# Load order, normalisation and transposes in the opening of a fused attention and feed-forward kernel

## The chip, the cores and the metric

The kernel runs on one core of one Trainium2 chip. The metric is the device time of one execution in microseconds (us), the median of several executions. The engines are PE (TensorE matmul), PEld (its weight load), DVE (VectorE), ACT (ScalarE), POOL (GpSimd) and SP, which here issues DMA transfers.

## The reference

Two rounds of a linear attention block and a bilinear feed-forward block, each on a layer norm of the residual stream (S = 2048 tokens, D = 1024, 32 heads, F = 3584):

```python
def _A_ref(x, wqkv, wo):                       # x: 1 x 2048 x 1024
    qkv = (x @ wqkv)                           # q, k, v; 32 heads of 32
    phi = lambda t: jnp.where(t > 0, t + 1, jnp.exp(t)) + 1e-6
    pq, pk = phi(q), phi(k)
    kv = jnp.einsum("bhsd,bhse->bhde", pk, v)  # one 32 x 32 matrix per head
    z = jnp.einsum("bhsd->bhd", pk)
    num = jnp.einsum("bhqd,bhde->bhqe", pq, kv)
    den = jnp.einsum("bhqd,bhd->bhq", pq, z)[..., None] + 1e-6
    return (num / den) @ wo
def _B_ref(x, w_gate, w_up, w_down):
    return ((x @ w_gate) * (x @ w_up)) @ w_down
x = x + _A_ref(_layernorm(x), wqkv, wo)
x = x + _B_ref(_layernorm(x), w_gate, w_up, w_down)
x = x + _A_ref(_layernorm(x), wqkv, wo)        # the same weights again
x = x + _B_ref(_layernorm(x), w_gate, w_up, w_down)
```

## The kernel before

A small scheduler records operations per engine. Every engine runs its own operations in the order in which they were recorded, and waits by semaphore for what an operation reads. So the order of the recording calls below is the program order of each engine. The 2048 tokens are 16 tiles of 128. The change touches only the opening of the first attention layer.

The loads go out in this order (`x0` in two halves comes first; a "half" of the key or query weights is 1 MB, a token tile 256 KB):

```python
load_w("k", 0)
xload(1)
load_w("k", 1)
xload(2)
load_w("q", 0)
xload(3)
load_w("q", 1)
for i in range(4, NST):
    xload(i)
```

The layer norm of one tile has three parts on DVE and POOL, and then its transposes:

```python
def ln_a(i):                      # statistics
    ...
    for h in range(2):
        P.add("dve", ... e.bn_stats(...) ...)      # half of the columns each
    P.add("dve", ... e.bn_aggr(...) ...)
    P.add("pool", ... add eps ...); P.add("pool", ... pow -0.5 ...)
    return j
# ln_b2: normalise, one tensor_scalar on DVE, f16 output
def transpose(self, n):
    if self.use_dma:
        P.add("sp", lambda e: e.dma_start_transpose(xnT[...], d), ...)
        return
    if self.to == "A0" and n == 0:                 # tile 0: two halves, two PSUM banks
        for hf, b in enumerate((B_TP, B_KQ[3])):
            P.add("pe", ... 4 transposes ...)
            P.add("act", ... e.copy(...) ...)
        return
    P.add("pe", ... 8 transposes ...)
    P.add("act", ... e.copy(...) ...)
```

The opening itself, and the loop over the first ten tiles' key and query projections (8 matmuls of 128x512 for each half):

```python
NHOLD = 2; NPL1 = 10; NPE_T = 6
def lnstep(i, h):                                  # called after key half h of tile i
    if h == 0:
        if lnp.n < NST:
            lnp.start(lnp.n)                       # statistics of one more tile
        lnp.b_one()                                # normalise one
    else:
        lnp.use_dma = i + 1 >= NPE_T               # later tiles: transposes by DMA
        lnp.step_t(1)                              # transpose one
lnp.start(0); lnp.b_one(); lnp.start(1); lnp.step_t(1); lnp.b_one(); lnp.start(2)
...
twk = tw_make("k", "dve", 1); twq = tw_make("q", "dve", 1)   # weight differences
seq = [("k", i) for i in range(NHOLD)]
for i in range(NHOLD, NPL):
    seq += [("q", i - NHOLD), ("k", i)]
...
for kind, i in seq:
    for h in range(2):
        ev = proj(kind, tok[i], h)                 # 8 matmuls on PE
        ev()                                       # exp, relu on ACT, combine on DVE
        if kind == "k":
            lnstep(i, h)
    if kind == "q" and i >= 1 and len(twk) > 1:
        twk.pop(0)()
    elif kind == "q" and i >= 1 and len(twq) > 1:
        twq.pop(0)()
    ...
```

The weight differences (`twk`, `twq`) are subtractions of weight blocks on DVE, 1.22 us each by the source view (the prediction reads 1.13 from the chain view). The next stage, which computes two tiles at a time with 7 block products in place of 8, reads them.

## Time and profile before

| | before |
|---|---|
| median of 3 runs | 1440.06 us (1439.99 to 1440.2) |
| span of the profiled run | 1438.3 us |
| PE busy | 1421.8 us, 16.5 us idle |
| first key product starts | 7.85 us |
| third key product starts | 14.74 us |
| first product of the next stage | 82.48 us |

Lines such as L891 are lines of the kernel. Between the two kernels they shift: the projections are L891 before and L907 after, the next stage L920 and L939, the transposes L546/L554 and L557/L565, the attention output L1242 and L1275, the gate and up products L1324 and L1357. Idle time in brackets is the idle time of that engine just before the group, and what is named after the arrow is what ended it. The clock in a table of stretches is that of PE, with 1.00 as full speed. The prediction below shows the lines of the profile and reads them.

### The profile page before, as it was taken

What the parts mean: (1) busy time and instruction counts of PE and PEld (TensorE: products, weight loads), DVE (VectorE), ACT (ScalarE), POOL (GpSimd) and SP (SyncE); (2) the same over time, 40 slices, a digit from 0 to 9 for tenths busy, and PEclk for the clock granted to TensorE, in tenths of its full rate; (3) what the DMA queues carried; (4) which work ended last, traced back from release to release, by engine and by line L of the source; (5) the groups of instructions that cost most, each with busy time, mean ns of one, the idle gap of its engine ahead of it and who ended that gap; (6) DMA issues with size and microseconds to landing.
All of it is one profiled execution on the core that took longest, in us unless ns stands there. A gap on an engine that the chain in (4) does not pass through costs nothing.

```text
span 1438.3 us, 21791 instructions
## 1 busy us (share of the span) xinstructions
PE 1421.8 (99%) x8126; PEld 787.8 (55%) x8186; DVE 1213.8 (84%) x2376; ACT 680.2 (47%) x1389; POOL 148.9 (10%) x176
## 2 busy tenths in 40 slices
PE   8999999999999999999999999999999999999999
PEld 3444444555545666664544444446666475666547
DVE  6987977999978799988779978778888887888888
ACT  5663255444420266662148823567776004777400
POOL 2212621000010000002000045310000100000000
PEclk9999999999999999999999999999999999999999
DMA  8477978997785777777984266757775976777653
GB/s 263 88 205 220 213 173 182 302 298 266 263 268 199 249 254 249 255 251 270 260 265 108 86 170 151 191 177 262 253 260 191 283 255 224 264 260 257 206 193 120
DMA packets 270458, 320.21 MB, mean 223 GB/s; under 512 B 161936, under 2 KB 212880, under 8 KB 270352
## 3 DMA queue, kind: packets, MB, share of 16 engines
q1 hardware_dynamic: 270352, 318.82, 72.2%
q8 instruction: 64, 1.05, 0.3%
q14 instruction: 42, 0.34, 0.1%
HBM read 236.45 MB, written 73.40 MB: 215 GB/s over the span
## 4 chain that ended last, share of the span: by engine, by line
PE 87%; DVE 7%; DMA 2%; issue 2%; ACT 1%; POOL 0%; SPq 0%; DVEq 0%; ACTq 0%
PE ps L1324 28%; PE ps L1741 17%; PE ps L1405 17%; PE ps L1140 8%; PE ps L920 6%; PE ps L1659 5%; PE ps L1242 4%; PE ps L891 3%; DVE arena L766 2%; DVE arena L451 1%; DMA arena<-arena 1%; DVE arena L769 1%; DVE arena L613 1%; DMA arena<-in_A_wqkv_dram 1%; PE ps L1166 0%
## 5 line engine op out<-in xcount | busy, mean ns | idle before, releaser
L766 DVE TENSOR_TENSOR arena<-arena 128x512 f16<-128x512 f16 (+8 forms) x1015 | 497.8, 518 | 59.8 <-ACT arena L1409 34.1
L1324 PE MATMUL ps<-arena 128*128 128x512 f16 x1888 | 457.2, 379 | 1.8 <-DVE arena L769 1.0
L769 DVE SCALAR_TENSOR_TENSOR arena<-ps,arena 128x512 f16<-128x512 f32 (+3 forms) x545 | 353.9, 664 | 69.4 <-PE ps L1741 28.4
L1405 PE MATMUL ps<-arena 128*128 128x256 f16 x2184 | 287.5, 273 | 1.0 <-DVE ps L1418 1.0
L1324 PEld LDWEIGHTS ps<-arena 128*128 128x128 f16 (+1 forms) x1888 | 182.9, 98 | 164.4 <-ACT ps L1353 3.8
L1405 PEld LDWEIGHTS ps<-arena 128*128 128x128 f16 (+1 forms) x2184 | 212.2, 98 | 91.6 <-ACT arena L1409 6.9
L1741 PE MATMUL ps<-arena 128*128 128x512 bf16 (+1 forms) x1102 | 242.6, 379 | 0.9
L1741 PEld LDWEIGHTS ps<-arena 128*128 128x128 f16 x1120 | 109.6, 98 | 130.2
L1329 ACT ACTIVATE arena<-ps 128x512 f32<-128x512 f32 x224 | 133.8, 597 | 76.5 <-PE ps L1324 61.7
L1409 ACT ACTIVATE arena<-ps 128x256 f32<-128x256 f32 x351 | 125.1, 384 | 26.9 <-PE ps L1405 22.0
L920 PE MATMUL ps<-arena 128*128 128x512 f16 (+1 forms) x551 | 122.4, 379 | 2.0 <-ACT arena L617 0.7
L1140 PE MATMUL ps<-arena 128*128 128x512 bf16 x498 | 114.7, 379 | 0.7
L1242 PE MATMUL ps<-arena 128*128 128x512 bf16 x502 | 110.5, 379 | 0.7 <-DVE arena L1248 0.2
L454 POOL TENSOR_SCALAR arena<-arena 128x1 f32<-128x1 f32 x64 | 24.8, 388 | 821.6 <-DVE arena L453 821.6
L1415 ACT COPY ps<-ps 128x256 f32<-128x256 f32 x182 | 66.3, 364 | 74.6 <-DVE arena L769 28.3
L1353 ACT COPY ps<-ps 128x512 f32<-128x512 f32 x112 | 65.4, 583 | 65.0 <-PE ps L1324 51.9
L451 DVE BATCH_NORM_STATS2 arena<-arena 128x6 f32<-128x512 bf16 x128 | 88.2, 689 | 8.9 <-DMA arena<-in_A_x_dram 6.7
L1022 POOL TENSOR_TENSOR arena<-arena 128x1024 f16<-128x1024 f32 x32 | 77.2, 2414 | 156.4 <-DVE arena L1020 142.0
L920 PEld LDWEIGHTS ps<-arena 128*128 128x128 f16 x560 | 53.9, 98 | 69.5 <-ACT arena L927 5.2
L891 PE MATMUL ps<-arena 128*128 128x512 bf16 x375 | 84.6, 379 | 4.2 <-ACT arena L556 1.6
L1659 PE MATMUL ps<-arena 128*128 128x256 f16 (+1 forms) x784 | 86.8, 273 | 0.3 <-ACT ps L1672 0.2
L1418 DVE TENSOR_TENSOR ps<-ps,arena 128x256 f32<-128x256 f32 x182 | 76.7, 428 | 10.5 <-PE ps L1405 9.5
(61 smaller groups left out, 905.9 us busy)
## 6 DMA issues: line engine op xcount, KB each, us to landing
arena<-w_scratch SPq DMA_DIRECT2D x84, 896.0 KB, 4.6
arena<-t_scratch SPq DMA_DIRECT2D x32, 896.0 KB, 5.8
arena<-in_B_w_down_dram SPq DMA_DIRECT2D x24, 896.0 KB, 4.9
arena<-sp_scratch SPq DMA_DIRECT2D x26, 768.0 KB, 4.3
w_scratch<-arena SPq DMA_DIRECT2D x28, 512.0 KB, 6.3
arena<-w_scratch SPq DMA_DIRECT2D x28, 384.0 KB, 5.0
x_scratch<-arena SPq DMA_DIRECT2D x40, 256.0 KB, 7.4
arena<-x_scratch SPq DMA_DIRECT2D x40, 256.0 KB, 5.9
```

The costliest lines, as they stand in the source:

```text
L766: P.add("dve", lambda e: e.tensor_tensor(out=out, in0=a, in1=b, op=op), rd=rd, wr=wr, prd=prd)
L769: P.add("dve", lambda e: e.scalar_tensor_tensor(out=out, in0=a, scalar=sc, in1=b, op0=ALU.mult, op1=op1), rd=rd, wr=wr, prd=prd)
L891: return [e.matmul(psb(bank), xnT[:, k, i * 128:(i + 1) * 128], t[:, k, h * 512:(h + 1) * 512], start=(k == 0), stop=(k == KT - 1)) for k ...
L920: P.add("pe", lambda e: [e.matmul(psb(bank), a[0][:, k, :], b[0][:, k, :], start=(q in (1, 5) and k == 0), stop=(k == 3), skip_group_check ...
L1140: return [e.matmul(psb(bank), xrt[t][:, jj * 128:(jj + 1) * 128], pk[:, h, t, :], start=(t == tok[0]), stop=(t == tok[NST - 1])) for t in ts]
L1242: return [e.matmul(psb(bank), xnT[:, g, i * 128:(i + 1) * 128], wp[:, g, dh * 512:(dh + 1) * 512], start=(dh == 0 and g == 0), stop=(g == ...
L1324: P.add("pe", lambda e: [e.matmul(psb(bank), w[:, k, :], x[:, k, :], start=(start and k == 0), stop=(k == 3), skip_group_check=True) for k ...
L1329: P.add("act", lambda e: e.activation(t, psb(bank), AF.Copy, scale=SG), prd=[bank], wr=r)
L1405: P.add("pe", lambda e: [e.matmul(psb(bank)[:, 256 * half:256 * half + 256], w[:, k, :], xx[:, k, :], start=(start and k == 0), stop=(k == ...
L1409: P.add("act", lambda e: e.activation(d, src, AF.Copy, scale=sc), prd=[xk], wr=rd_)
L1659: P.add("pe", lambda e: [e.matmul(psb(bank)[:, 256 * half:256 * half + 256], a[:, k, 128 * r:128 * r + 128], b[:, k, :], start=(start and ...
L1741: P.add("pe", lambda e: [e.matmul(psb(bank), hv[:, 7 * hf + k, t * 128:(t + 1) * 128], w[:, k, :], start=(q in "15" and hf == 0 and k == 0 ...
```

## The change

The intent: let PE transpose tile 1 while it would wait for the second half of the key weights anyway, keep a third key tile ahead of the first query product, give DVE work in its early idle time, and take the transposes of tiles 4 and 5 off PE. The core of the diff, with cuts:

```diff
-    NPE_T = 6
+    NPE_T = 4
...
+            def start_half(self):            # first half of a tile's statistics
+                return ln_a(self.order[self.n], None, (0,))
+            def start_rest(self, j):
+                ln_a(self.order[self.n], j, (1,))
...              # transpose(), tile 0
-                        P.add("act", ... e.copy(...)
+                        P.add(("act", "dve")[hf], ... (e.tensor_copy if hf else e.copy)(...)
...              # proj(): with mid, a call is made between k = 0..3 and k = 4..7
...              # lnstep()
                 if h == 0:
+                    if first and lnp.n < NST:
+                        for t in (lnp.n, lnp.n + 1):       # loads two tiles ahead
+                            if xnext[0] <= t < NST:
+                                xload(t)
+                                xnext[0] = t + 1
...              # the opening
                 lnp.start(0)
+                j1 = lnp.start_half()
                 lnp.b_one()
-                lnp.start(1)
                 lnp.step_t(1)
+                lnp.start_rest(j1)
                 lnp.b_one()
-                lnp.start(2)
...
-            for i in range(NHOLD, NPL):
-                seq += [("q", i - NHOLD), ("k", i)]
+                seq.append(("k", NHOLD))                   # three key tiles first
+            for i in range(NHOLD + 1, NPL):
+                seq += [("q", i - NHOLD - 1), ("k", i)]
...
+            lead = [[lambda: lnp.start(2), lambda: lnp.step_t(1)], [lambda: lnp.b_one()], [lambda: lnp.start(3)],
+                    [lambda: lnp.b_one()], [], [lambda: lnp.step_t(1)], [lambda: lnp.start(4)], [lambda: lnp.b_one(), lambda: lnp.start(5)]]
...
-                    ev = proj(kind, tok[i], h)
+                    ev = proj(kind, tok[i], h, (lambda: lnp.step_t(1)) if first and (kind, i, h) == ("k", 1, 1) else None)
                     ev()
-                    if kind == "k":
+                    if lead:
+                        for f in lead.pop(0):
+                            f()
+                        if i == NHOLD:
+                            twk.pop(0)()                   # weight differences earlier
+                    elif kind == "k":
                         lnstep(i, h)
-                if kind == "q" and i >= 1 and len(twk) > 1:
+                if kind == "q" and len(twk) > 1:
                     twk.pop(0)()
...              # loads
+        xload(1)
         load_w("k", 0)
-        xload(1)
         load_w("k", 1)
         xload(2)
         load_w("q", 0)
         xload(3)
         load_w("q", 1)
-        for i in range(4, NST):
-            xload(i)
+        xload(4)
+        xload(5)
```

The last lines also mean that tiles 6 to 15 are no longer loaded all at once at the start, but two tiles ahead of their statistics.

More of the change, by code (lines that the diff above doesn't have):

```diff
@@ L445, in build_kernel, with ln_a @@
         ln_cnt = [0]
-        def ln_a(i):
-            j = ln_cnt[0] % 8
-            ln_cnt[0] += 1
-            for h in range(2):
+        def ln_a(i, j=None, hs=(0, 1)):
+            if j is None:
+                j = ln_cnt[0] % 8
+                ln_cnt[0] += 1
+            for h in hs:
                 P.add("dve", (lambda h: lambda e: e.bn_stats(st[j][:, 6 * h:6 * h + 6], x_res[:, i, (D // 2) * h:(D // 2) * (h + 1)]))(h),
                       rd=r_x(i, (D // 2) * h, (D // 2) * (h + 1)), wr=R(O_ST[j] + 24 * h, 24))
+            if hs[-1] == 0:
+                return j
             P.add("dve", lambda e: e.bn_aggr(mv[j][:, 0:2], st[j]), rd=R(O_ST[j], 48), wr=R(O_MV[j], 8))
@@ L498, in start @@
                 self.q_b.append((i, j))
+            def start_half(self):
+                return ln_a(self.order[self.n], None, (0,))
+            def start_rest(self, j):
+                ln_a(self.order[self.n], j, (1,))
+                self.q_b.append((self.n, j))
+                self.n += 1
             def b1_one(self):
@@ L547, in transpose @@
                               rd=r + R(O_IDENT, 256), pwr=[b])
-                        P.add("act", (lambda hf, tq_: lambda e: e.copy(xnT[:, 4 * hf:4 * hf + 4, i * 128:(i + 1) * 128], tq_))(hf, tq_),
+                        P.add(("act", "dve")[hf], (lambda hf, tq_: lambda e: (e.tensor_copy if hf else e.copy)(xnT[:, 4 * hf:4 * hf + 4, i * 128:(i + 1) * 128], tq_))(hf, tq_),
                               prd=[b], wr=_seg(O_XT + 4 * hf * S * 2, 4, S * 2, i * 256, (i + 1) * 256))
@@ L861, in s_make, with xload @@
                                         (s3, a11, a21, ALU.subtract), (s4, a12, s2, ALU.subtract))]
+        xnext = [6]
+        def xload(i):
+            dma(x_res[:, i, :], x2[i * 128:(i + 1) * 128, :], r_x(i), KX[i])
         def layer_A(lnp, nxt, first):
@@ L883, in z_pair, with proj @@
                     tt(za, za, zt, ALU.add, rz_ + rt, rz_)
-            def proj(kind, i, h):
+            def proj(kind, i, h, mid=None):
                 t, v, c0, base = WSRC[kind]
@@ L888, in proj @@
                 kq_i[0] += 1
-                def fn(e):
-                    return [e.matmul(psb(bank), xnT[:, k, i * 128:(i + 1) * 128], t[:, k, h * 512:(h + 1) * 512],
-                                     start=(k == 0), stop=(k == KT - 1)) for k in range(KT)]
-                P.add("pe", fn, rd=r_xT(i * 128, (i + 1) * 128) + r_w(base, h * 512, (h + 1) * 512), pwr=[bank])
+                for ks in ((range(0, 4), range(4, 8)) if mid else (range(KT),)):
+                    P.add("pe", (lambda ks: lambda e: [e.matmul(psb(bank), xnT[:, k, i * 128:(i + 1) * 128], t[:, k, h * 512:(h + 1) * 512],
+                                                                start=(k == 0), stop=(k == KT - 1)) for k in ks])(ks),
+                          rd=r_xT(i * 128, (i + 1) * 128) + r_w(base, h * 512, (h + 1) * 512), pwr=[bank])
+                    if mid:
+                        mid()
+                        mid = None
                 def ev():
@@ L1052, in layer_A @@
             seq = [("k", i) for i in range(NHOLD)] if NPL else []
-            for i in range(NHOLD, NPL):
-                seq += [("q", i - NHOLD), ("k", i)]
-            seq += [("q", i) for i in range(max(NPL - NHOLD, 0), NPL if NPL < NST else 0)]
+            if NPL:
+                seq.append(("k", NHOLD))
+            for i in range(NHOLD + 1, NPL):
+                seq += [("q", i - NHOLD - 1), ("k", i)]
+            seq += [("q", i) for i in range(max(NPL - NHOLD - 1, 0), NPL if NPL < NST else 0)]
+            lead = [[lambda: lnp.start(2), lambda: lnp.step_t(1)], [lambda: lnp.b_one()], [lambda: lnp.start(3)],
+                    [lambda: lnp.b_one()], [], [lambda: lnp.step_t(1)], [lambda: lnp.start(4)], [lambda: lnp.b_one(), lambda: lnp.start(5)]]
             npack = [0]
@@ L1887, in build_kernel @@
         dma(x_res[:, 0, dh0:D], x2[0:128, dh0:D], r_x(0, dh0, D), KXB)
-        def xload(i):
-            dma(x_res[:, i, :], x2[i * 128:(i + 1) * 128, :], r_x(i), KX[i])
+        xload(1)
         load_w("k", 0)
-        xload(1)
         load_w("k", 1)
```

## The prediction

> **What bounds the kernel now.** I read the page's busy row first, then the slices, then the timeline of the tensor engine (PE) alone, and only then the waits inside the first 90 us, because the diff touches nothing but the opening of the first layer.
>
> The busy row of the page:
> ```profile
> PE 1421.8 (99%) x8126; PEld 787.8 (55%) x8186; DVE 1213.8 (84%) x2376; ACT 680.2 (47%) x1389; POOL 148.9 (10%) x176
> ```
> Against the span of 1438.3 us, PE is not busy for 16.5 us in all. Whatever the change does by taking idle time off PE, it cannot win more than that, 1.1%. The rest could only come from PE work removed. The slices say where the idle time is:
> ```profile
> PE   8999999999999999999999999999999999999999
> ...
> PEclk9999999999999999999999999999999999999999
> ```
> Only the first slice (0 to 36 us) is below 90%, and the clock is full throughout. The PE timeline of the first 100 us (start, length, operation; in brackets the idle time before and what ended it) shows the holes:
> ```profile
> 1.36 4.37 PE L431 MATMUL ps<-arena 128*128 128x512 f16 x10 [1.36 <-POOL arena L427]
> 6.28 0.62 PE L546 MATMUL ps<-arena 128*128 128x128 f16 x8 [0.55 <-DVE arena L471]
> 7.85 1.90 PE L891 MATMUL ps<-arena 128*128 128x512 bf16 x8 [0.94 <-ACT arena L548]
> 10.76 1.90 PE L891 MATMUL ps<-arena 128*128 128x512 bf16 x8 [1.01 <-DMA arena<-in_A_wqkv_dram]
> 12.49 0.61 PE L554 MATMUL ps<-arena 128*128 128x128 f16 x8
> 14.74 3.63 PE L891 MATMUL ps<-arena 128*128 128x512 bf16 x15 [1.64 <-ACT arena L556]
> ...
> 25.56 0.61 PE L554 MATMUL ps<-arena 128*128 128x128 f16 x8
> ...
> 40.71 36.42 PE L891 MATMUL ps<-arena 128*128 128x512 bf16 x165
> ...
> 82.48 1.03 PE L920 MATMUL ps<-arena 128*128 128x512 bf16 x4
> 83.83 3.00 PE L920 MATMUL ps<-arena 128*128 128x512 f16 x12 [0.33 <-DVE arena L766]
> 87.51 12.68 PE L920 MATMUL ps<-arena 128*128 128x512 f16 x57 [0.68 <-ACT arena L617]
> ```
> L431 is warm-up work, L546 and L554 are transposes of a token tile, L891 the projections, L920 the next stage. The first key product (7.85) waits for the copy of tile 0's transposes, the second (10.76) for the second half of the key weights, and the third (14.74) for the copy of tile 1's transposes, which were queued behind the second product. From 14.74 on PE runs without a gap to speak of until 77 us.
>
> The second place of loss is 82.48 to 87.51: 5.03 us for 16 products which at the undisturbed pitch (1.72 us for 8, from the key products above) take 3.45, so 1.58 us lost. The table of stretches says why:
> ```profile
> 50.00:80.00 30.00, 29.68 (x136) 13.40 (x138) 28.71 (x65) 17.66 (x35) 8.15 (x13) 1.00 0.64 131
> 15.00:50.00 35.00, 34.79 (x184) 16.84 (x187) 29.28 (x67) 23.61 (x41) 7.88 (x12) 1.00 0.53 151
> ```
> The third pair is DVE: 96% busy from 50 to 80 us, 84% from 15 to 50. DVE enters the next stage with a backlog, and PE waits on it and on ACT behind it. After 87.5 us the waits of PE in the whole trace sum to under 5 us; everything later is PE work, so a shift of this opening passes through to the end.
>
> [...] 8 products take 1.90 us with a 0.38 us tail, 217 ns apart. So a tile's 8 transposes cost PE about 0.45 us, and 25.56 to 26.22 in the full trace (before the next products) confirms that order. [...] Here a whole tile (8 blocks) lands 3.0 to 5.3 us after its issue:
> ```profile
> DMA to landing us min/median/max: 3.0/4.2/5.3
> ```
> [...] k weights half 0 at 7.0 us (issue 1.71, 5.3 to landing), tile 1 at 7.7, k half 1 at 10.7, tile 2 at 11.4, q half 0 at 14.4, tile 3 at 15.1. That is 0.7 us per 256 KB tile and 3.0 per 1 MB half, one behind another.
>
> **The change part by part.**
>
> 1. Loads. Tile 1 goes ahead of k half 0. It then lands about 0.7 us behind tile 0, whose second half landed at 3.5: near 4.3. k half 0 moves from 7.0 to 7.7. k half 1, tile 2, q half 0 and tile 3 have the same bytes ahead of them as before and keep 10.7, 11.4, 14.4, 15.1. The first key product stood at 7.85, so the 0.7 us costs nothing by itself; there is no gain there either, since the new limit (7.7) sits just under the old one. Splitting tile 0's copies between ACT and DVE (was 1.07 us for two on ACT, 6.72 to 7.79) brings the copy to about 7.4 and is hidden behind the weights. First key product: 7.8.
>
> 2. Tile 1's transposes. Half of its statistics goes between tile 0's aggregate (ends 4.68) and tile 0's normalise (5.68), filling a wait for POOL; it needs tile 1 by about 4.95, and has it at 4.3. The other half follows the DVE copy, 7.5 to 8.2, aggregate 8.25, and by the old spacing (aggregate 9.18, normalise 10.39) the normalise at 9.5 to 10.0. Its transposes run at 10.05 to 10.5, now inside the wait for k half 1 rather than after it. The second key product stays at 10.76. ACT does exp and relu of the first product (9.78 to 10.87) and then the copy (1.02 us), done at 11.9. So the third key product starts at 10.76 + 1.72 = 12.5 instead of 14.74: 2.25 us won (the 1.64 wait, 0.45 of transposes, the rest the pipeline tail).
>
> 3. Third key tile before the first query. q half 1 lands at 18.1, and the two products of key tile 2 give the queries until 20.6; without them the earlier PE would run into it. Tile 2's normalise: its load is at 11.4, two DVE evacuations lie around it, so 14.2 to 14.7. Its transposes sit in the middle of the fourth key product (15.1); ACT's copy queues behind exp and relu of the third (14.4 to 15.5), so 15.7 to 16.75, while PE is ready at 16.4. I charge 0.35 us. The number of products is the same as before.
>
> 4. Transposes of tiles 4 and 5 leave PE: 2 x 0.45 = 0.9 us. (ACT also loses two copies of 1.02 us.) By program order tile 4 is normalised after the second query half. Following DVE's queue by the old pitches (0.7 us an evacuation, 1.58 a tile's statistics, 0.41 a normalise, 1.13 a weight difference) that is at 27.1, and with 4.0 us of DMA the tile is there at 31.1; PE wants it at 31.0. Tiles 5 and 6 have about 1 us in hand (36.5 against 37.9, 44 against 44.8). I charge 0.2 us on average.
>
> 5. DVE. Work is the same but for one small copy; but the weight differences move from queries 1 to 6 to keys 2 and queries 0 to 3. Followed through, DVE hardly idles between 12 and 75 us, where it had some 6 us of real waits. It should finish the projections' work about 3 to 4 us earlier, PE about 2.8. So the loss at the entry of the next stage stays near 1.6 us or shrinks a little: 0.3 us.
>
> Sum: 2.25 - 0.35 + 0.9 - 0.2 + 0.3 = 2.9 us. After the shift everything else is the same instructions in the same order. 1440.06 - 2.9 gives about 1437.1.
>
> **The rivals.**
> - DMA transposes late: DVE lags by 5 to 7 us between 25 and 55 us in my account, so tiles 4 to 7 arrive when PE wants them or a little after. If the lag is 2 us worse, each may stop PE for 1 to 2 us. For it: 4.2 us landing, and the 96% row. Against it: PE's waiting lets DVE catch up, so the stops do not add, and time lost here is partly time that would be lost at the stage's entry anyway. The time would be 1438 to 1440.
> - DVE is the real bound up to 87 us: then the 2.25 us won at the front is given back where PE waits for DVE, and what counts is only how much of DVE's early idle time is filled. For it: the chain of waits runs through DVE from 46 to 76 us. If DVE finished only 1 us earlier, 1439; if it used all its waits, up to 4.5 us, 1435.5.
> - Tile 1 lands later than 4.95 and the half statistics hold back tile 0's normalise: all of the opening slips by that amount, but the weights at 7.7 and 10.7 stay the limit, so up to 0.7 us costs nothing. 1437 to 1438.
>
> **Range and chances.** The ceiling is 16.5 us of PE idle time, most of it not touched, so 2% (28.8 us) faster is out of reach; 2% slower would need a stall ten times any that I can construct. The least I expect is about 1 us (DVE bound), the most 4.6 (full relief at the stage's entry): 1435.4 to 1438.9, with 1437.1 in it. Within 2%: 98%; 1% each for the others.
>
> **What would show each step.** In the PE timeline of the changed kernel: tile 1's transposes between the first and second key product, and the third key product at 12.5 (step 2); the second still near 10.76 and released by the weights (step 1); under 0.5 us of wait after tile 2's transposes (step 3); 32 transposes in place of 48 there and no wait for a DMA at keys 4 to 7 (step 4); the next stage's first products near 79.5 and its dense run starting 2.5 to 3.5 us before 87.51 (step 5). A dense run beginning at 87 or later would make the DVE rival right; waits on the transposing DMA the first one. A shift at 87 us that is not found again at the end would show that something later absorbs it, and would make the prediction wrong in its last step.

The sum is 2.25 - 0.35 + 0.9 - 0.2 + 0.3 = 2.9 us. Its 0.45 us for a tile's 8 transposes stands without its working, but the trace of the kernel before shows it: the transposes start 56 ns apart, and the next product starts 0.45 us after the first of them (18.20 and 18.65 us). The 7.4 us for tile 0's copy in step 1 used an estimate of 0.4 us for a copy on DVE, and it is in no term of the sum. That loads come in time in the order of their issue is, as the prediction stands, a reading of the six landings that it lists. "The clock is full throughout" is the clock row of the page; the first clock record of that trace starts at 5.53 us, and the warm-up products before it start 427 ns apart.

## The result, and the profile after

The changed kernel took 1436.74 us, median of four runs (1435.71 to 1437.96). The kernel before took 1440.03 us in the same rounds (1439.48 to 1440.2). The ratio is 0.9978, with a 95% interval of 0.9961 to 0.9995. A ratio here is the mean time of one kernel's fast runs over that of the other's of the same rounds, so it is not quite the ratio of the medians. The median lies 0.4 us from the forecast, but the profile does not look like the forecast. The profiled run was the slowest of the four.

The busy row of the page of the changed kernel:

```profile
PE 1421.7 (99%) x8110; PEld 787.9 (55%) x8170; DVE 1212.8 (84%) x2377; ACT 677.0 (47%) x1386; POOL 148.5 (10%) x176
```

PE has 16 instructions fewer, the transposes of tiles 4 and 5, and yet it is as busy as before. Something made other PE work longer. The PE timeline of the first 100 us of the changed kernel (start, length, operation, idle time before it) shows it:

```profile
6.33 0.62 PE L557 MATMUL ps<-arena 128*128 128x128 f16 x8 [1.24 <-DVE arena L474]
9.79 3.57 PE L907 MATMUL ps<-arena 128*128 128x512 bf16 x8 [2.85 <-DVE arena L474]
13.16 1.06 PE L565 MATMUL ps<-arena 128*128 128x128 f16 x8
14.01 4.71 PE L907 MATMUL ps<-arena 128*128 128x512 bf16 x19
18.56 0.61 PE L565 MATMUL ps<-arena 128*128 128x128 f16 x8
...
20.27 3.63 PE L907 MATMUL ps<-arena 128*128 128x512 bf16 x16 [0.24 <-ACT arena L567]
23.73 0.61 PE L565 MATMUL ps<-arena 128*128 128x128 f16 x8
24.18 58.87 PE L907 MATMUL ps<-arena 128*128 128x512 bf16 x266
82.89 17.31 PE L939 MATMUL ps<-arena 128*128 128x512 bf16 x77
```

The first key product starts at 9.79 us, not at 7.8, after 2.85 us of idle time, and takes 3.57 us in place of 1.90. The transposes of tile 1 follow it directly, as intended. The release named on the 9.79 line is a normalise on DVE; what really ended the wait is the first half of the key weights, which landed at 9.7 us (issued at 2.18, 7.5 us to landing, by the DMA view). From 24.18 us on there is one unbroken run of projections, and the next stage starts at 82.89 without a single listed wait.

The table of stretches (PE, PEld, DVE, ACT and POOL busy with instruction counts, then the granted clock, the DMA share and GB/s) says why the product was slow. Before:

```profile
5.00:10.00 5.00, 3.26 (x18) 1.15 (x16) 2.14 (x4) 1.29 (x3) 1.01 (x3) 1.00 1.08 362
```

After:

```profile
5.00:10.00 5.00, 0.92 (x10) 0.59 (x10) 2.60 (x6) 0.59 (x1) 1.40 (x4) 0.76 1.06 356
10.00:15.00 5.00, 5.00 (x20) 2.34 (x19) 0.71 (x3) 1.60 (x3) 0.00 (x0) 0.55 1.08 357
15.00:50.00 35.00, 34.55 (x170) 16.04 (x172) 31.88 (x71) 22.20 (x41) 8.23 (x14) 1.00 0.59 145
```

The clock was 0.76 and 0.55 here: the trace's clock records have PE at half speed from 7.64 to 14.47 us, which is 6.83 us; in one repetition below the stretch is 3.41. The products of 10.2 to 12.7 us start 427 ns apart, those of the first key product before 216. In the 3.41 us up to 7.64 PE had been busy for 1.49 us (the table under a4 has more). The bandwidth (356 GB/s against 362) is the same, so the weights were not late for want of bandwidth.

To see what each stretch contributed I matched PE's weight loads of two traces one by one, counted from the end, and took the difference of their start times. Against the profile of before, the first load of the next stage came 0.41 us *later* in the changed kernel; twenty loads further (88.16 us in before) it was 0.86 us earlier; at 252 us 2.02 us earlier; at the end 2.06 us earlier. So the opening lost time in this profile, the entry of the next stage won 1.27, and another 1.16 us came between 200 and 252 us, where nothing had been changed. The wait table of PE from 200 to 252 us (what waited, on what: us in total, times, longest) names it. Before:

```profile
PE ps L1324 <- DVE arena L769: 1.0, 1, 1.0
PE ps L1324 <- DVE arena L766: 0.8, 1, 0.8
PE ps L1242 <- DVE arena L1248: 0.2, 1, 0.2
```

After:

```profile
PE ps L1357 <- DVE arena L780: 1.0, 1, 1.0
```

Two waits on DVE are gone. They belong to a DVE operation on a block of 128x2048 which itself waits for a DMA transpose. That wait was 4.54 us in the DVE timeline of before:

```profile
229.68 1.23 DVE L766 TENSOR_TENSOR arena<-arena 128x2048 f16<-128x2048 f16 x1 [4.54 <-DMA arena<-arena]
```

It was 3.38 us in the DVE timeline of the changed kernel:

```profile
227.65 1.23 DVE L777 TENSOR_TENSOR arena<-arena 128x2048 f16<-128x2048 f16 x1 [3.38 <-DMA arena<-arena]
```

The transpose that it waits for took 5.1 us from issue to landing before and 3.5 after. In DVE's program order the operations that copy PE's results out of their banks (L1248) and those that prepare the next products (L766, L769) stand behind it, and PE waits for both (0.2, 0.8 and 1.0 us in the table of before). The size fits: DVE waited 1.16 us less, and PE gained 1.16 us between 200 and 252 us. The same holds in every other usable profile below in which the weight copies of that stage were left where they were: PE's shift in this stretch is the change of that one DVE wait, to within 0.02 us (c1 waited 3.00 us and gained 1.54; a3 waited 5.57 and lost 1.02; c4 waited 4.79 and lost 0.25).

### The profile page after: what moved, and what is told of

The parts are those of the page before. It is cut to its first block, busy times and chain, and to the rows that moved or that the text cites. A ratio compares the mean times of both kernels' runs of the same rounds, so it can differ in the third digit from the quotient of the medians.

```text
span 1436.2 us, 21761 instructions
## 1 busy us (share of the span) xinstructions
PE 1421.7 (99%) x8110; PEld 787.9 (55%) x8170; DVE 1212.8 (84%) x2377; ACT 677.0 (47%) x1386; POOL 148.5 (10%) x176
## 3 DMA queue, kind: packets, MB, share of 16 engines
q8 instruction: 64, 1.05, 0.3%
## 4 chain that ended last, share of the span: by engine, by line
PE 94%; DVE 4%; issue 1%; ACT 1%; DMA 0%; POOL 0%; DVEq 0%
PE ps L1357 28%; PE ps L1774 17%; PE ps L1438 17%; PE ps L1173 8%; PE ps L1275 7%; PE ps L907 6%; PE ps L939 6%; PE ps L1692 5%; DVE arena L777 2%; DVE arena L452 1%; PE ps L1199 1%; DVE arena L780 0%; PE ps L1226 0%; DVE arena L959 0%; DVE arena L624 0%
## 5 line engine op out<-in xcount | busy, mean ns | idle before, releaser
L777 DVE TENSOR_TENSOR arena<-arena 128x512 f16<-128x512 f16 (+9 forms) x1015 | 497.8, 518 | 59.5 <-ACT arena L1442 34.2
```

The costliest lines, as they stand in the source:

```text
L777: P.add("dve", lambda e: e.tensor_tensor(out=out, in0=a, in1=b, op=op), rd=rd, wr=wr, prd=prd)
```

## The experiments

The theory after this first look: the part with the loads is what costs, by late weights and by the half clock behind them; everything else works as meant or better. The rival: the loads are harmless and the profiled run was an unlucky one, and DVE alone decides what arrives at 88 us. A third theory concerns the 200 to 252 us stretch: DMA transposes decide it, not the opening.

All profiles below were read with the same matching of weight loads. The columns are the shift in us against the profile of before (negative is earlier), at the first weight load of the fourth product (16.26 us before; weight loads run up to 0.2 us ahead of their product, as 82.27 against 82.48 in before), at the next stage's first weight load (82.27), at the twentieth one after it (88.16), at 252 us and at the end; then the median, and the median minus that of the kernel before in the same session. One profile stands for one run, and the median for five (four for the first row).

| kernel | 4th product | 82 | 88 | 252 | end | median | less own before |
|---|---|---|---|---|---|---|---|
| forecast | -2.2 | -2.8 | -2.9 | -2.9 | -2.9 | 1437.1 | -2.9 |
| changed kernel, first look | +1.22 | +0.41 | -0.86 | -2.02 | -2.06 | 1436.74 | -3.3 |
| c1_again, the same | -0.21 | -1.02 | -2.29 | -3.83 | -3.41 | 1436.32 | -5.2 |
| a2_oldloads | -1.76 | -2.57 | -3.84 | -4.67 | -4.76 | 1435.67 | -5.1 |
| a3_filler | -1.64 | -2.20 | -3.46 | -2.45 | -2.23 | 1437.38 | -3.3 |
| a4_pe_transposes | -1.65 | -1.57 | -2.84 | -3.70 | -3.66 | 1437.21 | -3.5 |
| b1_before_npet | -0.17 | -1.06 | -1.06 | -2.27 | -1.57 | 1438.48 | -2.1 |
| b2_before_pack | +0.13 | +0.12 | +0.12 | -0.54 | +0.74 | 1440.00 | -0.6 |
| b3_late_differences | -1.34 | -1.90 | -1.71 | -3.55 | -3.21 | 1437.11 | -3.5 |
| b4_two_ahead | -1.23 | -2.38 | -3.64 | -5.19 | -5.01 | 1436.02 | -4.5 |
| c2_two_ahead_pack | -1.46 | -2.60 | -3.87 | -4.19 | -3.63 | 1436.95 | -4.5 |
| c3_before_differences | +0.90 | +0.57 | -0.70 | -0.25 | +1.42 | 1439.67 | -1.8 |
| c4_before_loads | +2.01 | +2.01 | +2.01 | +3.16 | +4.79 | 1441.05 | -0.4 |

The kernel before had medians of 1440.72, 1440.56 and 1441.47 us in the sessions of the a, b and c kernels. Every kernel gave a correct result. The 82 column takes the first weight load of the next stage in each kernel; counted from the end, four profiles (a4, b4, c2, c3) were one record out of step there, and the 1.05 us in the expectation of b3 comes from such a count.

### The unaltered changed kernel again (a1_again, c1_again)

No edit; the kernel ran twice more beside the others.

> The changed kernel once more, unaltered. In its first profile the first half of the key weights landed at 9.7 us, not at the forecast 7.7: the records of single packets show 15 of the 16 DMA engines done with it by 8.3 and one at 9.4. PE stood idle from 6.95 to 9.79 and then ran at half clock until 14.8. Theory A (the late engine comes with the new load order in every run): the landing is again past 9 us, the first key product again near 9.8, one or two stretches of half clock, median 1436 to 1437. Rival B (the late engine was an accident of that one run): landing near 7.7, first key product near 7.8, clock full, and the profiled execution near 1434.

One of the five executions of a1_again, the profiled one, ran at a clock of 0.625 and took 2253 us. It is a slow run and nothing is read from it. The other four took 1434.77 to 1436.35 us; the ratio of the fast runs is 0.9964 (0.995 to 0.9977).

> The changed kernel unaltered a third time, for a profile in an ordinary state (the second was taken while the chip ran at 0.63 of its clock). From the four profiles with the new load order: the first half of the key weights lands 6.1 to 7.5 us after an issue at 2.18, the second 8.6 to 10.0 after one at 2.71, so 8.3 to 9.7 and 11.3 to 12.7; with the old order 6.8 to 7.4 and 10.5 to 11.1. I expect 8.3 and 11.4 here, the first product at 8.4 to 8.6, and the next stage's dense run about 3.5 us before that of the kernel before if the clock stays full, about 1 us before if it halves. Median near 1436.5.

c1_again took 1436.32 us (1435.67 to 1436.58), ratio 0.9961 (0.9949 to 0.9974). Its PE timeline:

```profile
7.11 0.62 PE L557 MATMUL ps<-arena 128*128 128x128 f16 x8 [1.29 <-DVE arena L474]
8.97 3.25 PE L907 MATMUL ps<-arena 128*128 128x512 bf16 x8 [1.24 <-DMA arena<-in_A_wqkv_dram]
```

Here the key weights landed at 8.9 us, and the wait is openly put down to the DMA. The clock was at half speed for 3.41 us. Tile 1 landed only at 5.9 us, so its half statistics held back tile 0's normalise and the transposes stood at 7.11: the third rival of the prediction happened in this run. What follows: the late weights and the half clock are no accident of one profile, but their size differs by 1.4 us between two profiles of the same kernel.

### The old load order (a2_oldloads)

```diff
                 lnp.start(0)
-                j1 = lnp.start_half()
                 lnp.b_one()
                 lnp.step_t(1)
-                lnp.start_rest(j1)
+                lnp.start(1)
...
-        xload(1)
         load_w("k", 0)
+        xload(1)
```

> The changed kernel with the first half of the key weights again ahead of tile 1 and tile 1's statistics again in one piece after tile 0's copy (needed, else the statistics would hold back tile 0). Everything else as changed. Theory A: the weights land at 7.0, the first product starts near 7.8 and the clock stays full; tile 1's transposes come at about 11, so the third key product starts near 13.1 against 16 in the first profile of the changed kernel: the time falls by 2 to 3 us to about 1434. Rival B: no difference from the unaltered changed kernel, or 0.6 us slower, since by plan the new order was worth 0.6 us.

The edit also puts tile 1's statistics back in one piece, so it undoes two things. It took 1435.67 us (1434.86 to 1436.57), ratio 0.9963 (0.995 to 0.9975). Its PE timeline:

```profile
7.37 1.90 PE L907 MATMUL ps<-arena 128*128 128x512 bf16 x8 [0.52 <-DVE arena L559]
10.81 0.62 PE L565 MATMUL ps<-arena 128*128 128x128 f16 x8 [1.53 <-DVE arena L474]
11.26 4.48 PE L907 MATMUL ps<-arena 128*128 128x512 bf16 x19
...
79.91 20.33 PE L939 MATMUL ps<-arena 128*128 128x512 bf16 x91
```

The first product is early and fast, the third follows from 12.78 us on (its first weight load), and this opening is 3 us better than that of the changed kernel's first profile. The medians (1435.67 against 1436.2 in the same session) point the same way by 0.5 us, but the ranges overlap. The traces show the gain in the opening; the medians do not resolve it.

### PE kept busy while it waits (a3_filler)

```diff
                 lnp.step_t(1)
+                P.add("pe", lambda e: [e.matmul(psb(B_KVT[1]), wrm[:, 0:128], wrm, start=True, stop=True) for _ in range(10)],
+                      rd=R(O_A[0], 1024), pwr=[B_KVT[1]])
                 lnp.start_rest(j1)
```

> The changed kernel with 10 more idle products (zeros, into the warm-up bank, never read) between tile 0's transposes and the first key product: 2.2 us of PE work that ends near 9.1 us. Theory A (half clock is a consequence of the idle stretch before the first product): the clock stays full, products run at 216 ns, and although no weight lands earlier, the third key product starts near 13.5 rather than 16; total 1.5 to 2.5 us faster than the unaltered changed kernel. Rival (half clock comes from elsewhere, or the weights are the only limit): same time, or up to 1.4 us slower in executions where the weights land at 7.7.

The time was 1437.38 us (1436.91 to 1438.67), ratio 0.9975 (0.9963 to 0.9988). Its PE timeline:

```profile
6.96 2.32 PE L1066 MATMUL ps<-arena 128*128 128x512 f16 x10
9.12 1.89 PE L907 MATMUL ps<-arena 128*128 128x512 bf16 x8
...
230.78 7.08 PE L1277 MATMUL ps<-arena 128*128 128x512 bf16 x31 [1.21 <-DVE arena L1283]
```

With the idle time filled, the clock was full from before the first product, which took 1.89 us. That product starts later than it could (the weights were there at 8.3), because the filler blocks PE until about 9.1. Up to 88 us this version is 2.6 us ahead of the changed kernel's first profile. It loses 1.0 us between 200 and 252 us: DVE waited 5.57 us for the transpose there, which took 5.8 us, and PE then waited 1.21 us. The filler repairs the opening but shows no gain in the median.

### Six tiles transposed on PE (a4_pe_transposes)

```diff
-    NPE_T = 4
+    NPE_T = 6
```

> The changed kernel with the transposes of tiles 4 and 5 back on PE. My step 4: 2 x 0.45 us more PE work, less 0.2 to 0.3 us of a wait for the transposing DMA at key tile 4: 0.6 to 0.9 us slower than the unaltered changed kernel. Rival (DVE and ACT set the end of the projections, so PE work removed there is worth nothing): within 0.2 us.

The time was 1437.21 us (1436.32 to 1438.48), ratio 0.9977 (0.9964 to 0.9991), 1.0 us above the unaltered kernel of the session. Its PE timeline:

```profile
8.45 1.89 PE L907 MATMUL ps<-arena 128*128 128x512 bf16 x8 [1.45 <-DVE arena L456]
...
11.36 4.49 PE L907 MATMUL ps<-arena 128*128 128x512 bf16 x19 [0.58 <-DMA arena<-in_A_wqkv_dram]
```

The profile fell on a run in which the clock stayed full in spite of 1.45 us of idle time. So the half clock is not certain with the new load order: of its five usable profiles (the first look, a3, a4, c1, c4) three ran the first product at half clock, and the one with the filler and a4 did not.

In two of them the clock fell from full to half. PE's busy time in the 3.41 us before the fall (transposes included) was:

```
profile             clock fell at (us)   PE busy in the 3.41 us before it (us)   at half speed for (us)
changed kernel      7.64                 1.49                                    6.83
c1                  9.34                 0.99                                    3.41
```

The idle time just before the first product does not decide it alone: it was 2.85 us in the changed kernel and 1.24 in c1, where the clock fell, and 1.45 in a4, where it stayed full. With the filler of a3 it stayed full. By what rule the clock falls, and why a4 escaped, is not shown by any run.

### The kernel before with four tiles transposed on PE (b1_before_npet)

```diff
-    NPE_T = 6
+    NPE_T = 4
```

> The kernel before with only the transposes of tiles 4 and 5 moved to the DMA. My step 4 alone: 0.9 us of PE work gone; the key tiles come later here, so no wait for the DMA: the next stage's first product at 81.6 instead of 82.48. If the loss at that stage's entry (1.58 us before) is set by DVE, which this leaves alone, it grows by as much and the dense run still starts at 87.5: then 0 to 0.3 us in all. If not, 0.9 us faster.

It took 1438.48 us (1438.4 to 1438.98), ratio 0.9987 (0.9974 to 0.9999). The profile is 1.06 us ahead at the next stage, of which 0.17 is an earlier second product (10.59 against 10.76), so 0.89 us belong to the transposes. PE's timeline at the entry of the next stage still has both of the old waits:

```profile
82.77 3.00 PE L920 MATMUL ps<-arena 128*128 128x512 f16 x12 [0.33 <-DVE arena L766]
86.46 3.83 PE L920 MATMUL ps<-arena 128*128 128x512 f16 x17 [0.68 <-ACT arena L617]
```

So this part alone gives just the 0.9 us of PE time that it removes, and nothing at the entry.

### The weight copies moved in the kernel before (b2_before_pack)

In the attention output stage, which ends at about 240 us, pairs of DMA copies rearrange gate and up weights in pieces of 256 bytes. I moved one of these pairs away from the transpose that DVE waits for.

```diff
-                if first and i % 3 == 1:
+                if first and i in (1, 4, 5, 7, 13):
                     pack()
```

> The kernel before with one pair of weight copies between two DRAM areas (256-byte pieces) moved: not issued just ahead of the transposes of the late tiles of the first layer's end, but some 17 us earlier. In the traces the transposing DMA of the tile that DVE waits for there took 5.1 us to land in the kernel before, 3.5 in the changed one, 4.1 with the old load order and 5.8 with the filler, and PE lost 0.94, 0, 0.29 and 1.97 us at that spot. Theory (the copies stretch the landing): it lands in 3.0 to 3.6 us, DVE waits under 3.5 us instead of 4.54, and PE loses nothing there: 0.8 to 1.0 us faster than before. Rival (the landing is stretched by something else, or the wait moves elsewhere): same time.

It took 1440.0 us (1439.85 to 1440.74), ratio 0.9997 (0.9985 to 1.001). In the profile DVE's wait fell from 4.54 to 3.31 us and 0.66 us were won between 88 and 252 us, but 1.2 us were lost again at about 1150 us, at another place where PE waits for DVE. Between 200 and 252 us PE won 0.57 us less than DVE's wait fell, because it now waited for ACT there:

```profile
PE ps L1242 <- ACT ps L1236: 0.4, 1, 0.4
```

The median does not show a gain. Nor is it shown that the copies stretch the transpose: with the copies where they were, the same DVE wait is 2.71 to 3.38 us in the changed kernel, c1, b1, b3 and b4.

### The weight differences late again (b3_late_differences, against a2_oldloads)

```diff
-                        if i == NHOLD:
-                            twk.pop(0)()
...
-                if kind == "q" and len(twk) > 1:
+                if kind == "q" and i >= 1 and len(twk) > 1:
```

> The variant with the old load order, and the weight differences back at queries 1 to 6 as in the kernel before (so DVE has no such work at key tile 2). In that variant as in all the changed ones so far, 1.05 to 1.27 us of the 1.58 lost at the entry of the stage after the projections had gone. Theory (DVE gets its work done earlier because the differences fill its early waits): most of that gain, about 1 us, goes again, and the dense run of the next stage starts about 1 us later than in the variant. Rival (it comes from the order of keys and queries, which leaves three queries without a tile's statistics at the end): unchanged within 0.3 us.

It took 1437.11 us (1436.58 to 1437.59), ratio 0.9976 (0.9963 to 0.9989). Its PE timeline at the entry of the next stage:

```profile
82.12 1.04 PE L939 MATMUL ps<-arena 128*128 128x512 f16 x4 [0.52 <-DVE arena L777]
83.66 1.90 PE L939 MATMUL ps<-arena 128*128 128x512 f16 x8 [0.50 <-ACT ps L942]
85.81 14.40 PE L939 MATMUL ps<-arena 128*128 128x512 f16 x65 [0.24 <-DVE arena L694]
```

The waits at the entry are back, and even one on a weight difference itself (L694). From the next stage's first load to the twentieth this kernel loses 0.19 us more than before did, where a2 wins 1.27. DVE was busy for 30.17 us of the stretch from 15 to 50 us here, 31.88 in the changed kernel and 29.28 before.

### Keys of two tiles ahead in place of three (b4_two_ahead, against a2_oldloads)

```diff
-            if NPL:
-                seq.append(("k", NHOLD))
-            for i in range(NHOLD + 1, NPL):
-                seq += [("q", i - NHOLD - 1), ("k", i)]
+            for i in range(NHOLD, NPL):
+                seq += [("q", i - NHOLD), ("k", i)]
...      # the lead list shifted; tile 2's transposes after the fourth key product, not inside it
```

> The variant with the old load order, but the keys of only two tiles ahead of the first queries, as before; tile 2's transposes then follow the fourth key product. My step 3: the first query would start near 16.9, when its weights (14.4) are there, and its second half near 18.7, just after 18.1: so I expect no wait for weights here, nor the 0.24 us of wait after tile 2's transposes. What changes is the end: two queries rather than three after the last key. If the three-ahead order is what relieves the next stage's entry (the rival of the run before), 1 us slower than the variant; if the differences are, within 0.3 us.

It took 1436.02 us (1434.99 to 1437.55), ratio 0.9972 (0.9958 to 0.9986). Its PE timeline:

```profile
11.33 0.62 PE L565 MATMUL ps<-arena 128*128 128x128 f16 x8 [1.93 <-DVE arena L474]
```

After that there is no gap of PE's down to the next stage, although the first queries come two products earlier. At 88 us it is 3.64 us ahead of before, a2 3.84. But it was 0.53 us behind a2 already at the fourth product, before the two orders part, because tile 1 had landed later (8.04 against 7.51 us). From the fourth product on it wins 2.41 us and a2 2.08. So the third key tile is not what makes the gain; with the old loads it earned nothing here.

### Both candidates together (c2_two_ahead_pack, against b4_two_ahead)

```diff
-                if first and i % 3 == 1:
+                if first and i in (1, 4, 5, 7, 13):
                     pack()
```

> The candidate: old load order, tile 1's transposes between the first two products, keys of two tiles ahead, early weight differences, transposes of tiles 4 and 5 by DMA, and the pair of weight copies moved as in the earlier run on the kernel before. Without the last it measured 4.5 us less than before. If the moved copies are worth their 0.8 us also here: 5 us less; if their gain is given back at the second layer, as in that run's profile, the same 4.5.

It took 1436.95 us (1436.37 to 1438.01), ratio 0.9967 (0.9955 to 0.998). Between 88 and 252 us its profile wins 0.3 us, b4's had won 1.55 without the move. PE waits 0.7 us for ACT there, as in b2. So moving the copies does not help here, and this candidate does not beat the changed kernel.

### Only the weight differences early, in the kernel before (c3_before_differences)

```diff
                         lnstep(i, h)
-                if kind == "q" and i >= 1 and len(twk) > 1:
+                        if i == NHOLD:
+                            twk.pop(0)()
+                if kind == "q" and len(twk) > 1:
                     twk.pop(0)()
```

> The kernel before with only the weight differences earlier: at query 0, at both halves of key tile 2 and from query 1 on, in place of queries 1 to 6. Nothing else. If they alone relieve the entry of the next stage: the loss there falls from 1.58 us to under 0.6 and the dense run starts near 86.4 instead of 87.5, all else equal: 1.0 us faster. If they need the other parts, unchanged.

It took 1439.67 us (1438.5 to 1441.44), ratio 0.9983 (0.9969 to 0.9996). Its PE timeline at the entry has no wait up to the end of the stretch that I looked at, 90 us:

```profile
83.05 7.17 PE L920 MATMUL ps<-arena 128*128 128x512 bf16 x31
```

So the earlier differences alone win 1.27 us at the entry (from +0.57 to -0.70), with nothing else changed, and 0.33 us before it (from +0.90 at the fourth and tenth product to +0.57). This profile lost 0.9 us near 183 us and 1.6 us near 1150 to 1170 us, where DVE held PE up.

### Only the loads changed, in the kernel before (c4_before_loads)

```diff
-        load_w("k", 0)
         xload(1)
+        load_w("k", 0)
         load_w("k", 1)
```

> The kernel before with only tile 1's load moved ahead of the first half of the key weights. By the plan in the prediction: the first product still at 7.8, the second at 10.76, nothing gained or lost. By what the profiles showed: the weights land at 8.3 and 11.4, the second product starts 0.6 us later than before and everything behind it too: 0.6 us slower, more in executions with a late DMA engine, and with it half clock in some.

It took 1441.05 us (1440.13 to 1444.79), ratio 0.9999 (0.9986 to 1.0012). The profiled run was the slowest of the five, 3.7 us above its median, so its shifts overstate the cost. Its PE timeline:

```profile
8.48 6.19 PE L891 MATMUL ps<-arena 128*128 128x512 bf16 x16 [0.84 <-DMA arena<-in_A_wqkv_dram]
```

The first two products, 16 matmuls, took 6.19 us at half clock (the trace's first record of the full clock starts only at 13.72 us). By the medians the load order alone gains nothing and costs nothing that five runs could show; by the trace it starts the first product 0.6 us later and can start it at half clock.

### What the transfers did

The trace has 16 completion signals for each of these loads, and the load counts as landed with the last of them (in the changed kernel that was at 9.66 us, and the first product started at 9.79). The trace does not name the source of a signal; that each stands for one DMA engine, as the expectations of a1 and c4 have it, is a reading of mine. The ends of single packets, which the expectation of a1 quotes, lie 0.1 to 0.3 us earlier. For the first half of the key weights, in us:

```
                           first signal   15th        16th        spread (us)
before                     6.53           6.87        7.02        0.49
seven others, old order    6.34-6.86      6.75-7.61   6.83-7.91   0.33-1.05
changed kernel             7.30           8.37        9.66        2.36
four others, new order     7.22-7.34      7.76-8.69   8.27-8.84   1.00-1.52
```

In the changed kernel the last signal was 1.3 us behind the fifteenth, and so it was again in the next loads: of the signals of tile 2's load fifteen came by 12.06 us and the last at 13.35. The landings of the eight profiles with the old order and the five with the new one do not overlap. The spreads just do: c3, with the old order, has 1.05 us, a3 and c4, with the new one, 1.00. So a wide spread is more common with the new order but not confined to it, and why a 256 KB tile ahead of the weights should spread the signals is not shown by any run.

## Why the prediction was right or wrong

The total was right: 1436.74 us measured against 1437.1, inside the range of 1435.4 to 1438.9. The three measured gains (3.3, 4.5 and 5.2 us against the kernel before of the same rounds) lie at and above the forecast 2.9. But the total came out right by luck, because terms that were sized too high and too low offset each other.

- **Loads (step 1): the step that failed.** It said that half 0 of the key weights moves from 7.0 to 7.7 us and half 1 keeps 10.7, at no cost. The five profiles with the new order have 8.3 to 9.7 for half 0 and 11.3 to 12.7 for half 1. The argument added up bytes and took the order of issue as the order in time. For the first of the 16 signals that was right (6.53 us before, 7.30 after); the last moved by 2.64 us. That a transfer's place in the issue order is its place in time was not shown beyond the landings of the kernel before, which lie one behind another (7.0, 7.7, 10.7, 11.4, 14.4 and 15.1 us). The second half of the failure, the clock, was in no step and in no rival: PE idled 2.85 us before the first product and then ran it at half speed, 3.57 in place of 1.90 us, so 1.67 us from that alone.
- **Tile 1's transposes (step 2): right in mechanism, spoilt by step 1.** The third key product was forecast at 12.5 us, a gain of 2.2. Its weight loads began at 12.78 in a2 and at 12.88 in a4, where the clock was full, and the fourth product there was 1.76 and 1.65 us earlier than before. So the place between the products is worth about 1.7 us. (The new copy on DVE took 0.42 us; the estimate of 0.4 was near it.) In the changed kernel's first profile the fourth product was 1.22 us later than before, and in c1 0.21 us earlier.
- **Third key tile (step 3): the size of the charge about right, the part itself not needed.** The wait for ACT's copy after tile 2's transposes was 0.24 us against a forecast of 0.35; with the restart behind it, 0.41 us went from the fourth to the tenth product, in the first profile and in a2 alike. But b4 shows that two tiles ahead do as well or better.
- **Transposes by DMA (step 4): right.** Forecast 0.9 less 0.2. The working cites 25.56 to 26.22 us, which is 0.66, for its 0.45; the two tiles removed do show 0.45 each (32.91 to 33.36 and 40.26 to 40.71). b1 measured 0.89. The 8 transposes of a tile last 0.61 us on PE, to the end of the last; one DMA transpose of a tile's 8 blocks landed 3.1 to 6.2 us after its issue in the changed kernel. In the changed kernel a weight load waited 0.29 us at 34.50 us for the DMA transpose, but PE itself has no listed wait for a DMA at keys 4 to 7, so the 0.2 was not needed, and the first rival did not happen.
- **DVE and the entry of the next stage (step 5): much too small.** Forecast 0.3 us. Measured 1.26 to 1.27 at the entry in all eight profiles with the early differences (the changed kernel twice, a2, a3, a4, b4, c2, c3); c3 has it with nothing else changed, and b3 lacks it. Another 0.33 us before the entry comes from them too: c3 has it alone, b3 only 0.08. I had noticed that DVE would use some 6 us of idle time, and yet let only 0.3 us of that reach PE. DVE was 91% busy from 15 to 50 us (31.88 of 35) against 84% before. So the second rival, in its version "if it used all its waits", was nearer to the truth than the main account, with 1.6 us and not the whole of it.
- **"A shift of this opening passes through to the end" (the last step): failed.** Between 88 and 252 us another 0.8 to 1.8 us came in the profiles of the changed kernel, a2, a4, b1, b3 and b4, 0.7 in b2, only 0.3 in c2, and in a3 1.0 us went, in c3 0.45 and in c4 1.15 (both lost 0.9 near 183 to 185 us). PE there waits for DVE, which waits for a DMA transpose whose landing varies (3.5 us after the change, 4.1 in a2, 5.1 before, 5.8 in a3); what stretches it is not shown. A second such place at about 1150 us cost b2, c3 and c4 1.2 to 1.6 us. Part of this is from run to run, since two profiles of the same changed kernel differ by 0.4 us there and by 1.4 us at the opening. I had read "the waits of PE after 87.5 us sum to under 5 us" as "nothing can move there"; 5 us was more than the whole gain in question.

The sum for the changed kernel's first profile, from the matched weight loads: +1.22 (fourth product) +0.41 (tile 2's copy and the restart, up to the tenth product) -0.89 (transposes of tiles 4 and 5, taken from b1) -0.33 (the earlier differences up to the next stage, taken from c3) makes the +0.41 found there; then -1.27 at the entry, -1.16 near 230 us and -0.04 after. For a2 the first four terms are -1.76, +0.41, -0.89 and -0.33, which makes its -2.57. The later loads of tiles 6 to 15 are not needed for this sum.

What is open: why the signals spread, more often with the new order; by what rule the clock falls; what sets the landing of the transpose near 228 us; and how much of the 200 to 252 us gain comes from the change and how much from chance. The version with the lowest median is a2, the change with the old load order: 1435.67 us. It is 0.5 us below the unaltered changed kernel of its session, with overlapping ranges, and equal to that of the last session when each is taken against its own before (5.1 and 5.2 us). So no version was shown to beat the changed kernel.

## What to carry to other kernels

A transfer that the first matmul needs should go out first: a small transfer ahead of it can cost more than its bytes (in before tile 1 landed 0.7 us behind the key weights; with tile 1 ahead of them they landed 2.64 us later), because the load counts as landed only with the last of its signals (9.66 us, the fifteenth at 8.37), and the idle time of PE near the start may be paid a second time in half clock (3.57 us for the first product in place of 1.90). The traces show this; the medians of the two orders differ too little to. Idle time of a second engine early on is worth filling even when it is not the bound there: subtractions moved forward by a few products took 1.27 us off a place 60 us later. When the whole gain in question is 3 us, a sum of waits of 5 us elsewhere is not nothing, and each of those waits has to be read before a shift is said to pass through.
